# Chunk-by-chunk pooling on GpSimd, side-by-side halves of the mixed attention tiles, and another PSUM layout for the last stage of attention, MoE and a second feed-forward layer

## Chip, cores and metric

The kernel runs on one core of one Trainium2 chip. The metric is the device time of one execution in microseconds; the time before is the median of three runs. One further execution was recorded by the hardware profiler, and every duration below comes from it.

## The reference, cut to what matters

```python
k_p = k.reshape(B, H, Sp, 8, D).mean(axis=3)      # 8 batches, 8 heads, 576 rows -> 72
v_p = v.reshape(B, H, Sp, 8, D).mean(axis=3)
scores = scale * (q @ k_p^T)                      # 576 x 72 for each batch and head
x = softmax(scores) @ v_p                         # -> 4608 tokens x 512
e = argmax(cosine(x, expert_emb) / tau)           # one of 8 experts per token, gate = its softmax weight
x = gate * (relu(x @ w1[e]) @ w2[e])              # first MoE, 512 -> 1024 -> 512
out = max(x @ m1, x @ m2, x @ m3) @ m_out         # second layer, 512 -> 768 -> 512
```

All of it is in float32.

## The kernel before

The work has three stages, and one written order of instructions for each engine. **Attention** goes over 36 tiles of 128 tokens. In a group of nine, tiles 0 to 3 belong to one batch, tile 4 (the mixed one) takes 64 tokens of one batch and 64 of the next, and tiles 5 to 8 belong to the second batch; so tiles 4, 13, 22 and 31 are mixed. An iteration of the loop works on several tiles at once: scores of one (`psc`, L422 and L436), transposed weights of an older one (`paT`, L467), transposed queries of the newest (`pqT`, L411), and weights times V of the oldest (`pav`, `stage_x`, L490). Each of `psc`, `paT` and `pav` has one PSUM buffer, so the next tile's matmuls wait until VectorE or ScalarE has read the last one's.

K and V of a batch come as 576 rows of 8 x 64, in five chunks (four of 128 partitions, one of 64), `kraw` and `vraw`. They are pooled in place in three halving steps, w = 4, 2, 1. For K of batches 0 and 1 VectorE does it; the rest is GpSimd's: `pool_k2` (L263) for K of batches 2 to 7 and `pool_v` (L275) for V of all eight. The four full chunks are done together at each step, `pool_v` taking its first step in two halves, and then the fifth. `spread_v` (L284, instructions at L288) then copies pooled V into the block form `vbd` that `pav` reads. All this stands in one GpSimd queue, and with it the one-hot rows `ohs` (`slot_steps`, L652, L656) of the routing.

The routing's small VectorE instructions (`rank_steps`, L600, through the helpers at L547 to L559 and the copy at L617) are put between the attention's own by `fill` (L910), a few at each place. A chain of them starts after tiles 8, 17 and 23, and another after the last. `early_steps` (L703) multiplies the `ohs` of the first 24 tiles into a list of tokens (`p_early`, L751), with which the first gather of the MoE starts.

**The first MoE** runs over pairs of blocks of 128 tokens of one expert; its matmuls are split in two parts (`hi`, `lo`) of a faster format. **The second layer** (`second`, L1568) takes six groups of 768 tokens, for each of which nine weight chunks go through seven products (`quad`, L1662, matmuls at L1617) in three PSUM tags of the pool `pabc` (L1573), and then an output product into the pool `pout` (L1574). In the first two stages the pools `pq` and `pb` (L117, L118) take PSUM: two banks for `pq`, then six for `psc`, `paT` and `pav`. The last result of the first MoE goes from `paT`'s banks through a transpose into one of `pq`'s (`pyT`, L1126).

Of the kernel before, what the change touches and what calls it, by code (L numbers as in the profile page):

```python
# [14 lines left out]
A = mybir.AluOpType  # L15
AX = mybir.AxisListType.X
PSUM = bass.MemoryType.PSUM
# [4 lines left out]
def attention_moe_moe_kernel(  # L22
# [24 lines left out]
    nc = tc.nc  # L47
    dbg = dbg or {}

    P = 128  # L50
# [38 lines left out]
    def pool(stack, name, bufs, side="left", space=None):  # L89
        kw = {"space": space} if space else {"side": side}  # L90
        return stack.enter_context(tc.tile_pool(name=name, bufs=bufs, reuse_waits="tile", **kw))
# [19 lines left out]
    def bc(ap, shape):  # L111
        return ap.to_broadcast(shape)
# [3 lines left out]
    if True:  # L116
# [61 lines left out]
        if True:  # L178

            RC = [P, P, P, P, 64]  # L180
# [67 lines left out]
            def prep_steps(b):  # L248
                kt, vt = kv[b]
                kb, vb = kbds[b % 3], vbds[b % 3]  # L250
                kp = qp.tile([P, 5, 2, D], F32, tag="kp", name=f"kp{b}")
                vp = kp[:, :, 1, :] if b > 1 else qp.tile([P, 5, D], F32, tag="vp", name=f"vp{b}")
# [8 lines left out]
                        pool_k(c)  # L261

                def pool_k2():  # L263
                    for c0, c1, n in ((0, 4, P), (4, 5, RC[4])):
                        for w in (4, 2, 1):
                            dst = kt[0:n, c0:c1, 0:w, :] if w > 1 else kp[0:n, c0:c1, 0:1, :]
                            nc.gpsimd.tensor_tensor(
                                dst, kt[0:n, c0:c1, 0:w, :], kt[0:n, c0:c1, w : 2 * w, :], op=A.add
                            )

                def dup_k():
                    for c0, c1, n in ((0, 3, P), (3, 4, KC[3]), (4, 5, KC[4])):
                        nc.scalar.copy(kp[0:n, c0:c1, 1, :], kp[0:n, c0:c1, 0, :])

                def pool_v(c0, c1, n):  # L275
                    for w in (4, 2, 1):
                        for a0 in range(c0, c1, 2) if w == 4 else (c0,):
                            a1 = min(a0 + 2, c1) if w == 4 else c1
                            dst = vt[0:n, a0:a1, 0:w, :] if w > 1 else vp[0:n, a0:a1, :].unsqueeze(2)
                            nc.gpsimd.tensor_tensor(  # L280
                                dst, vt[0:n, a0:a1, 0:w, :], vt[0:n, a0:a1, w : 2 * w, :], op=A.add
                            )

                def spread_v():  # L284
                    for c, (h0, h1) in enumerate(HS):
# [188 lines left out]
            AV = []  # L474
# [7 lines left out]
            def stage_x(i):  # L482
                m, part, t, segs = tiles[i]
                aT = st_a.pop(i)
                ps = pb.tile([P, 2, 512], F32, tag="pav", name=f"pav{i}")
                for lo, hi, b in segs:
                    for bank in range(2):
                        parts = [x_ for x_ in AV if x_[1] // 4 == bank]
                        for n, (c, g0, g1, sl) in enumerate(parts):
                            nc.tensor.matmul(  # L490
                                ps[lo:hi, bank, (g0 % 4) * DA : (g0 % 4 + g1 - g0) * DA],
                                aT[0 : RC[c], c, lo:hi],
                                vbds[b % 3][0 : RC[c], sl : sl + g1 - g0, :].rearrange("p h d -> p (h d)"),
                                start=(n == 0),
                                stop=(n == len(parts) - 1),
                                skip_group_check=True,
                            )
                av = ps[:, :, 0 : 4 * DA].rearrange("p a (h d) -> p a h d", d=DA)
                rs = ap2.tile([P, 2, 4, 1], F32, tag="rs", name=f"rs{i}")
                nc.vector.tensor_scalar_add(rs, av[:, :, :, D : D + 1], J * 1e-9)  # L500
                fill(FILL[dense[0]][2])
                nc.vector.reciprocal(rs, rs)
                fill(FILL[dense[0]][3])
                if part == 1 or t % 2 == 0:
                    xg[i] = ap2.tile(
                        [P, 1 if part == 1 else 2, DM], F32, tag=f"x{part % 2}", name=f"x{i}", bufs=2 if part == 1 else 3
                    )
                    xg[i + 1] = xg[i]
                x = xg.pop(i)
                nc.vector.tensor_tensor(  # L510
                    x[:, t % 2, :].rearrange("p (a h d) -> p a h d", a=2, h=4), av[:, :, :, 0:D], bc(rs, [P, 2, 4, D]), op=A.mult
                )
                dt = ap2.tile([P, 2, 4, E], F32, tag="dt", name=f"dt{i}")
                fill(FILL[dense[0]][4])
                nc.vector.tensor_tensor(dt, av[:, :, :, D + 1 : DA], bc(rs, [P, 2, 4, E]), op=A.mult)
                fill(FILL[dense[0]][5])
                nc.vector.tensor_reduce(
                    lg[:, i, :].unsqueeze(2), dt.rearrange("p a h e -> p e (a h)"), axis=AX, op=A.add
                )
                fill(FILL[dense[0]][6])  # L520
                sq = ap1.tile([P, DM], F32, tag="sq", name=f"sq{i}")
                squares.append(
                    lambda: nc.scalar.activation(sq, x[:, t % 2, :], AF.Square, accum_out=ssq[:, i : i + 1])
                )
                if part == 1:
                    r0 = 2 * S * m + 512
                    nc.sync.dma_start(xbuf[r0 : r0 + P, :], x[:, 0, :])
                elif t % 2 == 1:
                    r0 = 2 * S * m + (0 if part == 0 else 640)
                    nc.sync.dma_start(  # L530
                        xbuf[r0 : r0 + 4 * P, :].rearrange("(p t) d -> p (t d)", t=4)[:, (t - 1) * DM : (t + 1) * DM],
                        x.rearrange("p t d -> p (t d)"),
                    )
# [376 lines left out]
            def fill(n=1):  # L910

                for _ in range(n):
                    free = [c_ for c_ in queue[0] if c_.state is None] if queue else []
                    if not free:
                        return
                    c_ = free[0]
                    queue[0].remove(c_)
                    queue[0].append(c_)
                    c_.step()
                    if c_.state == "end":  # L920
                        queue[0].remove(c_)
                        if not queue[0]:
                            queue.pop(0)
# [553 lines left out]
            for it in range(NT + 4):  # L1477
# [33 lines left out]
                if 0 <= it - 4 < NT:  # L1511
                    stage_x(it - 4)
                if it == NT + 1:
                    next(first)
                for job in todo.get(it, []):
# [3 lines left out]
                    b, j = job  # L1519
# [48 lines left out]
    def second(st, groups, again=False):  # L1568
        wq = pool(st, "wstream", 3)
        yp = pool(st, "yin", 2)  # L1570
        t2 = pool(st, "tmp2", 2)
        g1p = pool(st, "gT", 1)
        pa = pool(st, "pabc", 2, space=PSUM)  # L1573
        po_ = pool(st, "pout", 2, space=PSUM)  # L1574
        tl["yr"] = yp
        ghi, glo = (g1p.tile([P, F2C, GW], F32R, name=f"{x_}{groups[0]}") for x_ in ("ghi", "glo"))
        wt, gt, ix = {}, {}, {}
# [162 lines left out]
    with ExitStack() as st:  # L1740
        second(st, list(range(NG)))
# [61 lines left out]
```

## Time and profile before

| | |
|---|---|
| time before, median of 3 runs | 1264.73 us (1262.85 to 1265.89) |
| the profiled execution's own time | 1260.98 us |
| its span, first to last instruction | 1259.2 us |
| TensorE busy | 1215.6 us (97%) |
| VectorE busy | 799.2 us (63%) |
| ScalarE busy | 580.5 us (46%) |
| GpSimd busy | 318.9 us (25%) |
| granted TensorE clock, mean | 0.991 |

PE is TensorE's matmuls, PEld its weight loads, DVE VectorE, ACT ScalarE, POOL GpSimd and SP the engine that issues most DMAs. Attention fills about the first 205 us, the first MoE goes to 701 us, the second layer to the end. A view by window gives the busy time of each engine in a stretch; the timeline lists the instructions in order of time, equal neighbours merged, with the idle time before them and what ended it in square brackets. Of a merged row the time is from the start of its first instruction to the end of its last. A float32 matmul is recorded as two.

### The profile page before, as it was taken

What the parts mean: (1) busy time and instruction counts of PE and PEld (TensorE: products, weight loads), DVE (VectorE), ACT (ScalarE), POOL (GpSimd) and SP (SyncE); (2) the same over time, 40 slices, a digit from 0 to 9 for tenths busy, and PEclk for the clock granted to TensorE, in tenths of its full rate; (3) what the DMA queues carried; (4) which work ended last, traced back from release to release, by engine and by line L of the source; (5) the groups of instructions that cost most, each with busy time, mean ns of one, the idle gap of its engine ahead of it and who ended that gap; (6) DMA issues with size and microseconds to landing.
All of it is one profiled execution on the core that took longest, in us unless ns stands there. A gap on an engine that the chain in (4) does not pass through costs nothing. (4 is left out here: it accounts for less than half of the span.)

```text
span 1259.2 us, 22318 instructions
## 1 busy us (share of the span) xinstructions
PE 1215.6 (97%) x8251; PEld 1158.0 (92%) x8251; DVE 799.2 (63%) x1575; ACT 580.5 (46%) x1040; POOL 318.9 (25%) x383
## 2 busy tenths in 40 slices
PE   5899899999999999999999999999999999999995
PEld 4788789999999999999999998998998998998994
DVE  6676886797889999898764446345445454454450
ACT  3466465545666676666655333323223323223221
POOL 6985553420212212222000302103103004004001
PEclk9899999999999999999999999999999999999998
DMA  9968246423976445844619666475564673773721
GB/s 252 267 202 236 97 138 217 151 85 32 298 262 226 164 143 203 283 151 137 207 51 350 241 238 242 160 262 205 207 239 182 220 264 153 258 263 124 253 108 52
DMA packets 98038, 246.21 MB, mean 196 GB/s; under 512 B 17100, under 2 KB 58106, under 8 KB 89858
## 3 DMA queue, kind: packets, MB, share of 16 engines
q1 hardware_dynamic: 84770, 189.09, 44.5%
q0 software_dynamic: 13152, 55.62, 13.3%
q8 instruction: 67, 1.10, 0.4%
q14 instruction: 49, 0.40, 0.1%
HBM read 252.23 MB, written 46.98 MB: 238 GB/s over the span
## 5 line engine op out<-in xcount | busy, mean ns | idle before, releaser
L1617 PE MATMUL p<-yhi,wt 128*128 128x384 f32 x1512 | 387.2, 336 | 0.0
L1617 PEld LDWEIGHTS p<-yhi,wt 128*128 128x128 f32 x1512 | 273.4, 188 | 0.6
L1617 PE MATMUL p<-ylo,wt 128*128 128x384 f32 x756 | 254.0, 336 | 0.0
L1625 ACT COPY s<-p 128x384 f32<-128x384 f32 x162 | 77.8, 480 | 221.1 <-PE p L1617 216.8
L1104 PE MATMUL py<-hhi,whi 128*128 128x256 f32 x576 | 164.6, 286 | 0.0
L1104 PE MATMUL py<-hhi,wlo 128*128 128x256 f32 x576 | 163.1, 283 | 1.6 <-DVE wlo L1036 1.6
L1056 PE MATMUL ph<-xhi,whi 128*128 128x256 f32 x576 | 163.8, 284 | 0.7 <-DVE hlo L1072 0.7
L1056 PE MATMUL ph<-xhi,wlo 128*128 128x256 f32 x576 | 163.0, 283 | 0.7 <-DVE wlo L1036 0.7
L1056 PE MATMUL ph<-xlo,whi 128*128 128x256 f32 x576 | 163.0, 283 | 0.0
L1104 PE MATMUL py<-hlo,whi 128*128 128x256 f32 x576 | 162.9, 283 | 0.0
L1617 PEld LDWEIGHTS p<-ylo,wt 128*128 128x128 f32 x756 | 142.1, 188 | 0.5
L1646 DVE TENSOR_TENSOR blk<-p,s 128x384 f32<-128x384 f32 x108 | 59.7, 553 | 113.9 <-PE p L1617 113.9
L1602 POOL DMA_INDIRECT gt<-gbuf,ix x26 | 37.0, 1424 | 312.1 <-DMA ix<-idbuf 305.7
L1104 PEld LDWEIGHTS py<-hhi,wlo 128*128 128x128 f32 x576 | 110.4, 192 | 1.8 <-DVE wlo L1036 1.8
L1056 PEld LDWEIGHTS ph<-xhi,whi 128*128 128x128 f32 x576 | 110.5, 192 | 1.2 <-DVE hlo L1072 0.9
L1056 PEld LDWEIGHTS ph<-xhi,wlo 128*128 128x128 f32 x576 | 110.5, 192 | 0.9 <-DVE wlo L1036 0.9
L1056 PEld LDWEIGHTS ph<-xlo,whi 128*128 128x128 f32 x576 | 110.5, 192 | 0.0
L1104 PEld LDWEIGHTS py<-hlo,whi 128*128 128x128 f32 x576 | 110.5, 192 | 0.0
L1104 PEld LDWEIGHTS py<-hhi,whi 128*128 128x128 f32 x576 | 110.4, 192 | 0.0
L1036 DVE TENSOR_TENSOR wlo<-w2raw,whi 128x1024 fp32r<-128x1024 f32 x84 | 102.2, 1221 | 8.8 <-ACT whi L1034 8.7
L1036 DVE TENSOR_TENSOR wlo<-w1raw,whi 128x1024 fp32r<-128x1024 f32 x67 | 81.8, 1220 | 27.6 <-ACT whi L1034 26.5
L1034 ACT CAST whi<-w2raw 128x1024 fp32r<-128x1024 f32 x88 | 91.8, 1044 | 7.7 <-PE py L1104 4.7
(316 smaller groups left out, 2280.8 us busy)
## 6 DMA issues: line engine op xcount, KB each, us to landing
wt<-wdram SPq DMA_DIRECT2D x51, 1792.0 KB
w1raw<-in_moe_w_dram SPq DMA_DIRECT2D x88, 512.0 KB
w2raw<-in_moe_w_dram SPq DMA_DIRECT2D x88, 512.0 KB
wdram<-wst POOLq DMA_DIRECT2D x9, 1792.0 KB
ybuf<-yo SPq DMA_DIRECT2D x40, 256.0 KB
cvraw<-in_moe_w_dram POOLq DMA_DIRECT2D x36, 256.0 KB
vraw<-in_v_dram SPq DMA_DIRECT2D x8, 1024.0 KB
xbuf<-x SPq DMA_DIRECT2D x16, 512.0 KB
```

The source lines that it names most:

```text
L1034: nc.scalar.copy(hi, src)
L1036: eng.tensor_tensor(lo, src, hi.bitcast(F32), op=A.subtract)
L1056: nc.tensor.matmul(ps[:, f, :], a_[:, c, fs], b_[:, c, :], start=(n == 0), stop=(n == 3 * DC - 1))
L1104: nc.tensor.matmul(py[:, c // 2, (c % 2) * 256 : (c % 2 + 1) * 256], a_[:, f, c * P : (c + 1) * P], b_[:, f, :], start=(piece == 0 and f = ...
L1602: nc.gpsimd.indirect_dma_start(out=gt[g][:, j : j + 1], out_offset=None, in_=gbuf[:, :], in_offset=bass.IndirectOffsetOnAxis(ap=cols[j], a ...
L1617: nc.tensor.matmul(ps, a_, b_, start=(start and c + n == 0), stop=(c == 1 and n == 2), skip_group_check=True)
L1625: nc.scalar.copy(t, ps)
L1646: tt(src, add[0], add[1], op=A.add)
```

## The change

Three edits. `pool_k2` and `pool_v` now finish one chunk (three steps on at most 128 partitions x 256 elements) before the next. `stage_x` has its loop over the two halves of a mixed tile innermost, so that the halves alternate, and a tile with one batch keeps its order. `second` opens the pool `pout` ahead of `pabc`, so that `pout` takes PSUM's first two banks and `pabc` the other six.

```diff
--- before.py
+++ after.py
@@ -261,25 +261,20 @@
                         pool_k(c)
 
                 def pool_k2():
-                    for c0, c1, n in ((0, 4, P), (4, 5, RC[4])):
+                    for c, n in enumerate(RC):
                         for w in (4, 2, 1):
-                            dst = kt[0:n, c0:c1, 0:w, :] if w > 1 else kp[0:n, c0:c1, 0:1, :]
-                            nc.gpsimd.tensor_tensor(
-                                dst, kt[0:n, c0:c1, 0:w, :], kt[0:n, c0:c1, w : 2 * w, :], op=A.add
-                            )
+                            dst = kt[0:n, c, 0:w, :] if w > 1 else kp[0:n, c, 0:1, :]
+                            nc.gpsimd.tensor_tensor(dst, kt[0:n, c, 0:w, :], kt[0:n, c, w : 2 * w, :], op=A.add)
 
                 def dup_k():
                     for c0, c1, n in ((0, 3, P), (3, 4, KC[3]), (4, 5, KC[4])):
                         nc.scalar.copy(kp[0:n, c0:c1, 1, :], kp[0:n, c0:c1, 0, :])
 
                 def pool_v(c0, c1, n):
-                    for w in (4, 2, 1):
-                        for a0 in range(c0, c1, 2) if w == 4 else (c0,):
-                            a1 = min(a0 + 2, c1) if w == 4 else c1
-                            dst = vt[0:n, a0:a1, 0:w, :] if w > 1 else vp[0:n, a0:a1, :].unsqueeze(2)
-                            nc.gpsimd.tensor_tensor(
-                                dst, vt[0:n, a0:a1, 0:w, :], vt[0:n, a0:a1, w : 2 * w, :], op=A.add
-                            )
+                    for c in range(c0, c1):
+                        for w in (4, 2, 1):
+                            dst = vt[0:n, c, 0:w, :] if w > 1 else vp[0:n, c : c + 1, :]
+                            nc.gpsimd.tensor_tensor(dst, vt[0:n, c, 0:w, :], vt[0:n, c, w : 2 * w, :], op=A.add)
 
                 def spread_v():
                     for c, (h0, h1) in enumerate(HS):
@@ -483,10 +478,10 @@
                 m, part, t, segs = tiles[i]
                 aT = st_a.pop(i)
                 ps = pb.tile([P, 2, 512], F32, tag="pav", name=f"pav{i}")
-                for lo, hi, b in segs:
-                    for bank in range(2):
-                        parts = [x_ for x_ in AV if x_[1] // 4 == bank]
-                        for n, (c, g0, g1, sl) in enumerate(parts):
+                for bank in range(2):
+                    parts = [x_ for x_ in AV if x_[1] // 4 == bank]
+                    for n, (c, g0, g1, sl) in enumerate(parts):
+                        for lo, hi, b in segs:
                             nc.tensor.matmul(
                                 ps[lo:hi, bank, (g0 % 4) * DA : (g0 % 4 + g1 - g0) * DA],
                                 aT[0 : RC[c], c, lo:hi],
@@ -1570,8 +1565,8 @@
         yp = pool(st, "yin", 2)
         t2 = pool(st, "tmp2", 2)
         g1p = pool(st, "gT", 1)
+        po_ = pool(st, "pout", 2, space=PSUM)
         pa = pool(st, "pabc", 2, space=PSUM)
-        po_ = pool(st, "pout", 2, space=PSUM)
         tl["yr"] = yp
         ghi, glo = (g1p.tile([P, F2C, GW], F32R, name=f"{x_}{groups[0]}") for x_ in ("ghi", "glo"))
         wt, gt, ix = {}, {}, {}
```

GpSimd's queue, at the pooling of K of batch 2 (`kraw` and its result in `kp`), with the semaphores waited for: first before, whole, then the change, its first four chunks of five.

```order
L267 TENSOR_TENSOR kraw_254<-kraw_254 128x4x256 [waits DMAHW4_49,DMAHW3_49,DMAHW5_49,DMAHW2_49,DVE_49]
L267 TENSOR_TENSOR kraw_254<-kraw_254 128x4x128 [waits Pool_49]
L267 TENSOR_TENSOR kp_484<-kraw_254 128x4x64 [waits PE_49,Pool_49]
L267 TENSOR_TENSOR kraw_254<-kraw_254 64x256 [waits DMAHW3_49]
L267 TENSOR_TENSOR kraw_254<-kraw_254 64x128 [waits Pool_49]
L267 TENSOR_TENSOR kp_484<-kraw_254 64x64 [waits Pool_49]
```

```order
L267 TENSOR_TENSOR kraw_262<-kraw_262 128x256 [waits DMAHW4_49,DMAHW3_49,DMAHW5_49,DMAHW2_49,DVE_49]
L267 TENSOR_TENSOR kraw_262<-kraw_262 128x128 [waits Pool_49]
L267 TENSOR_TENSOR kp_500<-kraw_262 128x64 [waits PE_49,Pool_49]
L267 TENSOR_TENSOR kraw_262<-kraw_262 128x256
L267 TENSOR_TENSOR kraw_262<-kraw_262 128x128 [waits Pool_49]
L267 TENSOR_TENSOR kp_500<-kraw_262 128x64 [waits Pool_49]
L267 TENSOR_TENSOR kraw_262<-kraw_262 128x256
L267 TENSOR_TENSOR kraw_262<-kraw_262 128x128 [waits Pool_49]
L267 TENSOR_TENSOR kp_500<-kraw_262 128x64 [waits Pool_49]
L267 TENSOR_TENSOR kraw_262<-kraw_262 128x256
L267 TENSOR_TENSOR kraw_262<-kraw_262 128x128 [waits Pool_49]
L267 TENSOR_TENSOR kp_500<-kraw_262 128x64 [waits Pool_49]
```

Six instructions became fifteen. Second and third steps wait for GpSimd's own instruction before them, and a chunk's first step does not. For V seven instructions became fifteen.

TensorE's queue, at `pav` of the first mixed tile, before and then in the change; `vbd_154` and `vbd_155` are the two batches, and so the two halves.

```order
L490 MATMUL pav_707<-vbd_154,aT_638 64x146
L490 MATMUL pav_707<-vbd_154,aT_638 64x219
L490 MATMUL pav_707<-vbd_154,aT_638 64x73
L490 MATMUL pav_707<-vbd_154,aT_638 64x146
L490 MATMUL pav_707<-vbd_154,aT_638 64x219
L490 MATMUL pav_707<-vbd_154,aT_638 64x73
L490 MATMUL pav_707<-vbd_155,aT_638 64x146
L490 MATMUL pav_707<-vbd_155,aT_638 64x219
L490 MATMUL pav_707<-vbd_155,aT_638 64x73
L490 MATMUL pav_707<-vbd_155,aT_638 64x146
L490 MATMUL pav_707<-vbd_155,aT_638 64x219
L490 MATMUL pav_707<-vbd_155,aT_638 64x73
```

```order
L485 MATMUL pav_757<-vbd_154,aT_688 64x146
L485 MATMUL pav_757<-vbd_155,aT_688 64x146
L485 MATMUL pav_757<-vbd_154,aT_688 64x219
L485 MATMUL pav_757<-vbd_155,aT_688 64x219
L485 MATMUL pav_757<-vbd_154,aT_688 64x73
L485 MATMUL pav_757<-vbd_155,aT_688 64x73
L485 MATMUL pav_757<-vbd_154,aT_688 64x146
L485 MATMUL pav_757<-vbd_155,aT_688 64x146
L485 MATMUL pav_757<-vbd_154,aT_688 64x219
L485 MATMUL pav_757<-vbd_155,aT_688 64x219
L485 MATMUL pav_757<-vbd_154,aT_688 64x73
L485 MATMUL pav_757<-vbd_155,aT_688 64x73
```

The same twelve matmuls stand there, and now each is followed by its counterpart of the other half. Nothing else moves on TensorE, and nothing on VectorE, ScalarE or SP.

## Rows read from the trace of the kernel before

**Rows 1.** The page's first part: busy time, share of the span, instructions.

```profile
PE 1215.6 (97%) x8251; PEld 1158.0 (92%) x8251; DVE 799.2 (63%) x1575; ACT 580.5 (46%) x1040; POOL 318.9 (25%) x383
```

**Rows 2.** Stretches: length, then busy PE, PEld, DVE, ACT, POOL; PEclk, DMA share, GB/s.

```profile
81.40:93.60 12.20, 9.56 (x80) 8.58 (x78) 11.42 (x28) 6.03 (x17) 9.96 (x13) 1.00 0.38 120
125.80:142.20 16.40, 11.57 (x81) 9.90 (x78) 15.94 (x25) 7.08 (x19) 15.69 (x21) 0.90 0.33 111
93.60:125.80 32.20, 32.20 (x242) 28.98 (x241) 21.79 (x61) 21.36 (x55) 17.65 (x23) 1.00 0.81 239
```

**Rows 3.** VectorE's groups by shape, 79 to 142 us: busy us, mean ns.

```profile
L547 DVE TENSOR_TENSOR pre<-pre 128x72 f32<-128x72 f32 x8 | 7.0, 872 | 0.0
L547 DVE TENSOR_TENSOR oh<-w,wm 128x72 f32<-128x72 f32 x2 | 4.4, 2176 | 0.0
L617 DVE COPY pre<-oh 128x72 f32<-128x72 f32 x2 | 4.0, 2000 | 0.0
L551 DVE TENSOR_SCALAR lg<-lg,rtau 128x72 f32<-128x72 f32 x2 | 1.6, 821 | 0.0
L556 DVE SCALAR_TENSOR_TENSOR wt<-lg,w 128x72 f32<-128x72 f32 x2 | 1.1, 570 | 0.1
...
L547 DVE TENSOR_TENSOR rk<-rk,oh 128x72 f32<-128x72 f32 x1 | 0.2, 223 | 0.0
```

**Rows 4.** VectorE's timeline, two instructions of the second rank chain: start, duration.

```profile
129.57 3.92 DVE L547 TENSOR_TENSOR oh<-w,wm 128x72 f32<-128x72 f32 x1
...
137.08 2.62 DVE L547 TENSOR_TENSOR pre<-pre 128x72 f32<-128x72 f32 x1
```

**Rows 5.** GpSimd's timeline: batch 2's pooling, and a spread with batch 7's.

```profile
35.42 3.69 POOL L267 TENSOR_TENSOR kraw<-kraw 128x1024 f32<-128x1024 f32 x2
...
39.88 1.25 POOL L267 TENSOR_TENSOR kraw<-kraw 64x256 f32<-64x256 f32 x2
41.20 0.31 POOL L267 TENSOR_TENSOR kp<-kraw 64x64 f32<-64x64 f32 x1
41.48 3.83 POOL L280 TENSOR_TENSOR vraw<-vraw 128x512 f32<-128x512 f32 x3
...
47.66 3.70 POOL L267 TENSOR_TENSOR kraw<-kraw 128x1024 f32<-128x1024 f32 x2
...
129.06 2.04 POOL L288 TENSOR_TENSOR vbd<-kp,mslot 128x128 f32<-128x128 f32 x5
131.06 3.67 POOL L267 TENSOR_TENSOR kraw<-kraw 128x1024 f32<-128x1024 f32 x2
```

**Rows 6.** TensorE's timeline: a mixed `pav`, a plain one; mixed scores, plain ones.

```profile
57.96 3.63 PE L490 MATMUL pav<-vbd,aT 128*64 128x146 f32 x24
...
112.43 2.00 PE L490 MATMUL pav<-vbd,aT 128*128 128x146 f32 x12
...
83.72 1.35 PE L422 MATMUL psc<-kbd,qT 128*64 128x144 f32 x16 [0.20 <-ACT qT L412]
...
115.42 1.25 PE L436 MATMUL psc<-kbd,qT 128*128 128x144 f32 x8
```

**Rows 7.** GpSimd's timeline, the one-hot rows, with the idle time before them.

```profile
107.76 7.04 POOL L656 TENSOR_SCALAR ohs<-iof,slot,tokid 128x128 f16<-128x128 f32 x9 [15.49 <-DVE slot L556]
...
156.38 0.79 POOL L656 TENSOR_SCALAR ohs<-iof,slot,tokid 128x128 f16<-128x128 f32 x1 [13.04 <-DVE slot L556]
...
174.19 4.99 POOL L656 TENSOR_SCALAR ohs<-iof,slot,tokid 128x128 f16<-128x128 f32 x6 [5.62 <-DVE slot L556]
```

**Rows 8.** TensorE's timeline: the matmuls that read the one-hot rows.

```profile
181.04 0.75 PE L751 MATMUL p_early<-ohbe,ohs 128*128 128x10 f16 x24
```

**Rows 9.** TensorE's timeline near the start: a wait for queries.

```profile
40.69 0.63 PE L411 MATMUL pqT<-ident,qgrp 128*128 128x128 f32 x4 [2.88 <-DMA qgrp<-in_q_dram]
```

**Rows 10.** TensorE's timeline where the second layer begins.

```profile
700.79 0.66 PE L1126 MATMUL pyT<-ident,yr 128*128 128x128 f32 x4 [0.68 <-ACT yr L1097]
701.33 0.41 PE L1617 MATMUL p<-yhi,wt 128*128 128x384 f32 x1
```

## The prediction, made before the changed kernel ran

> **What bounds the kernel now.** I began with the page's busy times: TensorE works 97% of the span [rows 1], 1215.6 of 1259.2 us, so there are 43.6 us of idle TensorE to win, and beyond that only shorter TensorE work. Then I took busy times by window over the attention. Between 93.6 and 125.8 us TensorE is busy all the time; in the two stretches beside it, it idles for 12.20 - 9.56 = 2.64 us and 16.40 - 11.57 = 4.83 us, and VectorE is the full engine there (11.42 of 12.20, 15.94 of 16.40) [rows 2]. In the second one the granted clock is 0.90: the 1.2 GHz level for about 3.3 us of the 16.4, after TensorE had waited, which costs half of 3.3, some 1.6 us more. Together the two stretches cost 9.1 us.
>
> What fills VectorE there? Its groups by shape answer: five kinds of small routing instructions, 16 in all on 128 x 72 elements, take 7.0 + 4.4 + 4.0 + 1.6 + 1.1 = 18.1 us, though one on the same shape takes 0.22 when nothing disturbs it [rows 3]. So 18.1 - 16 x 0.22 = 14.6 us are waiting that the profile books as work. The timelines of VectorE and GpSimd, side by side, say on whom: `oh` runs from 129.57 to 133.49 [rows 4], and GpSimd runs its five spread instructions from 129.06 to 131.06 and the first step of batch 7's K after them (two steps in 3.67 us) [rows 5]. VectorE got in where the second step had to wait for the first. A `pre` of 2.62 us in the same chain is another such case [rows 4]. I read this as a shared way into memory that GpSimd keeps through a run of instructions without a wait between them.
>
> **Pooling chunk by chunk.** The three steps of a fifth chunk, which has the new size of 256 elements a partition, go from 39.88 to 41.48, thus 1.60 us, the last of them 0.28 [rows 5]. In the changed order only a chunk's second and third step wait for the step before. Dividing the other 1.32 us by size, I estimate 0.8 and 0.5 us. A VectorE instruction then meets either a run of 0.28 + 0.8 = 1.08 us (a last step and the next chunk's first) or one of 0.5 us. For an instruction that comes at any moment the mean wait is (1.08 x 1.08 + 0.5 x 0.5) / (2 x 1.6) = 0.44 us, and 16 of them wait 7.0 us instead of 14.6. Before, TensorE saw 7.5 us of the 14.6 as idle time (2.64 + 4.83) and VectorE's own slack took the other 7.1. What is left would fit that slack if it were spread evenly; since it won't be quite, I leave TensorE 1.1 of the 9.1 us. **Gain 8.0 us.** The ends: 9.1 if nothing of it reaches TensorE; and a loss of 3.0 if each of the 16 meets the longest run (17.6 us against 14.6).
>
> The Trainium skill ("SBUF — State Buffer", its rules on the shared port pair) has it that whichever of VectorE and GpSimd starts first holds the pair for its whole instruction, and the other waits. By that, `oh` would have got in after one spread instruction and not after all of them and a pooling step, so the trace shows longer holding than the page. By the page's rule alone the mean wait would be 0.30 us, the whole 9.1 us would come back, and the sum below would be 1.1 us larger.
>
> The price is GpSimd's time. K of batch 2 took 41.48 - 35.42 = 6.06 us and V 47.66 - 41.48 = 6.18 [rows 5]; both become 5 x 1.60 = 8.0. Batch 0's V is hidden by the wait for batch 1's data; six times 1.94 for K and seven times 1.82 for V make 24.4 us. The cover is GpSimd's idle time ahead of the one-hot rows: 15.49 + 13.04 + 5.62 = 34.2 us [rows 7]. But those waits are for VectorE, and if attention comes 8.0 us and three mixed tiles (below, 1.5 each) earlier, 12.5 us of the cover go: 21.7 are left, and the last one-hot rows come 2.7 us late against the rest. They end at 174.19 + 4.99 = 179.18 and are read at 181.04 [rows 7, 8], which leaves 1.9. **Loss 0.8 us**, as a wait ahead of `p_early`; between 0 and 2.7. Nearer needs have more room: no other reader of pooled K and V comes within 5 us of GpSimd's later times, as I carried them along the timeline.
>
> The first V pooling also frees a buffer 1.8 us later, and behind that load on SP's queue stand the queries for which TensorE waits at 40.69 [rows 9]. The DMA engines are saturated then and hold earlier loads in their queues, so I put that at nothing; without that cover it would cost up to 1.8 us once.
>
> **Halves side by side.** A mixed `pav` takes 3.63 us for 24 records, a plain one 2.00 for 12 of twice the width: run one after the other, half as wide costs as much apiece [rows 6]. The scores of mixed tiles already alternate their halves, and there 16 records take 1.35 us where 8 plain ones take 1.25 [rows 6]: two matmuls on different halves run together, for 8% more. So the new `pav` should take 2.00 x 1.08 = 2.16, and save 1.47 in each of four tiles. VectorE waits for each mixed `pav`, and TensorE has work behind it, so the saving lies on the path. **Gain 5.9 us**; ends 0 (accumulating chains don't overlap) and 4 x 1.63 = 6.5.
>
> **The banks.** The first product of the second layer starts at 701.33, right behind the transpose that ends about then (700.79 plus 0.66) [rows 10], and it waits for nothing. The new place only lets other old tiles stand under the tags, all read by then, and no product uses a bank that it shares with a reader later. **Nothing**, either way; the 0.68 us wait ahead of the transpose stays.
>
> **The sum**: 8.0 - 0.8 + 5.9 = 13.1 us. Against the profiled execution's own 1260.98 that is 1247.9. That execution lies 3.75 us below the median of the runs shown, so for the median I take 1264.73 - 13.1 = **1251.6 us**.
>
> **Rivals.** *GpSimd becomes the bound* (slower). From 27 us until the one-hot rows it would hardly rest. 65 chunk triples stand in that line (five for each of 13 poolings), so 0.1 us more for a triple makes `p_early`, and all behind it, 6.5 us later. At 1.80 us instead of 1.60 the whole gain is gone, and at 2.0 the time is 1264.73 - 13.1 + 26 = 1277.6. Against it: the fifth chunk's triple is the same work on as many elements. For it: 30 ends of instructions per batch at which VectorE may step in, instead of 13.
>
> *The waits only spread out.* If contested instructions wait as long in sum as before, the pooling gains nothing and only the halves are left: 1264.73 - 5.9 = 1258.8. For it: GpSimd is busy longer, so more is contested. Against: runs of 2.4 us and more are what rows 4 show.
>
> *The halves don't overlap.* Then 8.0 us remain and GpSimd isn't late: 1256.7. For it: unlike the scores, these add up in one bank. Against it: mixed scores use the same halves of the array.
>
> *The change doesn't reach the end*: TensorE's time is taken up by VectorE or ScalarE soon after, 1264.7. Against it: behind 142 us TensorE is nearly always the one that others wait for.
>
> **Numbers.** Chances: the forecast 0.72, halves alone 0.10, pooling alone 0.09, GpSimd as bound 0.05, nothing 0.04. The first's own range goes from both full gains, 15.6 us, to half of them, 6.5. The range to state also takes in the two partial cases (up to 1258.8) and, at the low end, the 3.75 us by which one execution already lay below the median: 1264.73 - 15.6 - 3.75 = 1245.4. So 1245 to 1259, leaving out under 0.2. A measurement of this kernel tells about 0.2%, 2.5 us, from no change: faster 0.91, same 0.04, slower 0.05.
>
> **What would show it.** Right: the first four groups of rows 3 near 0.6 us a piece at most, both stretches of rows 2 with under 1 us of idle TensorE and clock 1.00, mixed `pav` near 2.2 us, K and V pooling 8.0 us each, `p_early` some 12 us earlier with at most a short wait for GpSimd, the second layer's part unchanged in length. Wrong: triples over 1.7 us, a long wait ahead of `p_early`, mixed `pav` still near 3.6, or VectorE's small instructions still above 1 us.

## The result and the profile after

In the first comparison the changed kernel takes 1249.16 us (median of 4 runs, 1247.23 to 1252.42) and the kernel before 1264.99 us (4 runs). The ratio is 0.988, with a 95% interval of 0.9852 to 0.9908: faster, by about 15.8 us. In the second comparison (`e6_changed_again`) it is 0.9881 (0.9858 to 0.9904). The profiled execution of the changed kernel took 1247.23 us with a span of 1245.5 us. The forecast was 1251.6 us (1245 to 1259).

The changed code is shorter, so the line numbers of the attention are 5 lower than before (`pav` L485, `psc` L417 and L431, `p_early` L746, GpSimd's `pool_k2` L267, `pool_v` L277, spread L283 and `ohs` L651, VectorE's helpers L542 to L554).

The first part of the changed kernel's page, busy time and instructions of each engine:

```profile
PE 1206.5 (97%) x8251; PEld 1151.5 (92%) x8251; DVE 794.2 (64%) x1575; ACT 580.5 (47%) x1040; POOL 339.3 (27%) x501
```

Against [rows 1], GpSimd has 118 instructions and 20.4 us more, and TensorE is 9.1 us less busy with the same number of instructions.

TensorE's timeline shows a mixed `pav`, a plain one, and the queries for which it waited before:

```profile
40.87 0.60 PE L406 MATMUL pqT<-ident,qgrp 128*128 128x128 f32 x4
...
54.87 1.86 PE L485 MATMUL pav<-vbd,aT 128*64 128x146 f32 x24
...
112.36 2.00 PE L485 MATMUL pav<-vbd,aT 128*128 128x146 f32 x12
```

The mixed tile's 24 records now take 1.86 us, less than the plain tile's 12 of twice the width. Before, they took 3.63 [rows 6]: 1.77 us less in each of four tiles. The queries' wait of 2.88 us [rows 9] is gone.

The windows that answer to the two stretches of [rows 2] (length, then busy PE, PEld, DVE, ACT, POOL; clock, DMA share, GB/s):

```profile
76.00:88.00 12.00, 11.80 (x97) 10.60 (x94) 9.84 (x29) 8.30 (x24) 10.82 (x23) 1.00 0.61 185
116.00:127.00 11.00, 10.80 (x90) 9.87 (x89) 9.73 (x29) 7.30 (x22) 9.98 (x21) 1.00 0.59 198
```

In each of them TensorE idles for 0.20 us where it had idled for 2.64 and 4.83, at full clock, though GpSimd pools beside it for nine tenths of the time. VectorE's groups by shape, 75 to 126 us, answer to [rows 3] (busy us, mean ns of one):

```profile
L542 DVE TENSOR_TENSOR pre<-pre 128x72 f32<-128x72 f32 x8 | 3.3, 414 | 0.0
...
L551 DVE SCALAR_TENSOR_TENSOR wt<-lg,w 128x72 f32<-128x72 f32 x2 | 1.0, 496 | 0.1
L612 DVE COPY pre<-oh 128x72 f32<-128x72 f32 x2 | 0.9, 441 | 0.0
...
L542 DVE TENSOR_TENSOR oh<-w,wm 128x72 f32<-128x72 f32 x2 | 0.6, 304 | 0.0
L546 DVE TENSOR_SCALAR lg<-lg,rtau 128x72 f32<-128x72 f32 x2 | 0.6, 289 | 0.0
```

The 16 instructions take 3.3 + 1.0 + 0.9 + 0.6 + 0.6 = 6.4 us instead of 18.1. With 0.22 us of work in each, as the prediction took it, 2.9 us of waiting are left of 14.6. (0.22 is the shortest `pre`. The shortest `oh`, copy and `wt` of these chains are 0.30, 0.32 and 0.37 us, in the changed kernel or in `e4_step_by_step` below, so some 0.7 us of either figure is work and not waiting.)

GpSimd's price shows in its timeline: one chunk of batch 4's V, and its last one-hot rows, with batch 7's spread ahead of them:

```profile
79.93 1.25 POOL L277 TENSOR_TENSOR vraw<-vraw 128x256 f32<-128x256 f32 x2
81.27 0.32 POOL L277 TENSOR_TENSOR kp<-vraw 128x64 f32<-128x64 f32 x1
81.54 1.26 POOL L277 TENSOR_TENSOR vraw<-vraw 128x256 f32<-128x256 f32 x2
...
153.56 6.24 POOL L651 TENSOR_SCALAR ohs<-iof,slot,tokid 128x128 f16<-128x128 f32 x8
159.78 2.06 POOL L283 TENSOR_TENSOR vbd<-kp,mslot 128x128 f32<-128x128 f32 x5
161.84 4.93 POOL L651 TENSOR_SCALAR ohs<-iof,slot,tokid 128x128 f16<-128x128 f32 x6
```

A triple takes 81.54 - 79.93 = 1.61 us. Of the idle time that stood ahead of the one-hot rows [rows 7] nothing is left in these rows. VectorE and TensorE at the same time:

```profile
159.71 2.16 DVE L548 TENSOR_SCALAR texc<-texc 128x8 f32<-128x8 f32 x1
```

```profile
159.10 2.07 PE L485 MATMUL pav<-vbd,aT 128*128 128x146 f32 x12 [0.46 <-DVE pinc L554]
...
164.07 1.17 PE L417 MATMUL psc<-kbd,qT 128*64 128x144 f32 x14 [2.84 <-DVE sh L449]
...
168.04 0.83 PE L746 MATMUL p_early<-ohbe,ohs 128*128 128x10 f16 x24
```

`texc`, 128 x 8 elements, is held from 159.71 to 161.87 us, just as long as the spread of batch 7 lasts (159.78 to 161.84). Behind it on VectorE come the instructions for the softmax, and TensorE waits 2.84 us for them. Before, these scores had no wait above 0.38 us.

Where the time came from is best read as the lead of the changed kernel over the one before, at the same instruction of the two TensorE timelines:

| instruction on TensorE | before, us | after, us | lead, us | what happened since the line above |
|---|---|---|---|---|
| `pav` of tile 3 | 52.81 | 49.72 | 3.1 | the start: no wait for queries, no slow clock after it (see the text) |
| `pav` of tile 11 | 93.60 | 86.25 | 7.4 | mixed tile 4: 1.8; first stretch of rows 2: 2.5 |
| `pav` of tile 20 | 142.16 | 126.38 | 15.8 | mixed tile 13: 1.8; second stretch: 6.7 |
| `pav` of mixed tile 22, start | 150.98 | 135.13 | 15.9 | |
| `p_early` | 181.04 | 168.04 | 13.0 | mixed tile 22: 1.8; the last routing chain: -4.6 |
| first product of the first MoE | 205.50 | 191.10 | 14.4 | mixed tile 31: 1.8; slow clock left from the waits: -0.4 |
| first product of the second layer | 701.33 | 687.24 | 14.1 | |
| last instruction | 1259.2 | 1245.5 | 13.7 | |

So the gain is 3.1 (start) + 7.1 (four mixed tiles) + 9.2 (two stretches) - 5.0 (last chain and its aftermath) = 14.4 us by the end of attention, of which 13.7 last to the end. The first of these terms is not the change's alone: the start also differs between two executions of the same attention (see the start, under the experiments). The medians differ by some 2 us more than the two profiled executions: before's profiled one lay 4.0 us below its median, after's 1.9.

### The profile page after: what moved, and what is told of

Its sections match the earlier page's. It is cut to its first block, busy times and chain, and to the rows that moved or that the text cites. A ratio compares the mean times of both kernels' runs of the same rounds, so it can differ in the third digit from the quotient of the medians.

```text
span 1245.5 us, 22435 instructions
## 1 busy us (share of the span) xinstructions
PE 1206.5 (97%) x8251; PEld 1151.5 (92%) x8251; DVE 794.2 (64%) x1575; ACT 580.5 (47%) x1040; POOL 339.3 (27%) x501
## 3 DMA queue, kind: packets, MB, share of 16 engines
q0 software_dynamic: 13152, 55.62, 13.4%
```

## The experiments

The theory under test: small VectorE instructions come to a shared way into memory only where GpSimd has to wait for its own previous instruction; chunk by chunk, such a wait comes at every second and third step. Each experiment starts from the kernel before or the changed one, and the ratio is always to the kernel before, measured beside it.

**One part at a time.** `e1_pool_alone` is the kernel before with the new `pool_k2` and `pool_v` alone, its other lines as they were:

```diff
                 def pool_k2():
-                    for c0, c1, n in ((0, 4, P), (4, 5, RC[4])):
+                    for c, n in enumerate(RC):
                         for w in (4, 2, 1):
...
                 def pool_v(c0, c1, n):
-                    for w in (4, 2, 1):
-                        for a0 in range(c0, c1, 2) if w == 4 else (c0,):
+                    for c in range(c0, c1):
+                        for w in (4, 2, 1):
...
```

> Only the pooling is chunk by chunk; mixed halves and banks as before. My theory (GpSimd keeps the shared way through a run of instructions without a wait, short triples let VectorE in): the two stretches after tiles 8 and 17 lose their 2.64 and 4.83 us of idle TensorE and the clock returns to 1.00 there (9.1 us), the wait for queries near 40 us with the slow clock behind it goes as in the changed kernel (3.1 us), and because attention reaches the one-hot rows 5 us later than in the changed kernel, less is lost there: 1265 - 12 = 1253 us, between 1251 and 1256. Rival (the halves did most of it, the waits only spread out): 1260 or more.

Measured: 1250.14 us against 1264.95, ratio 0.9872 (0.9827 to 0.9917), a little below the expected 1251 to 1256.

`e2_halves_alone` is the kernel before with the new loop order of `stage_x` alone:

```diff
-                for lo, hi, b in segs:
-                    for bank in range(2):
-                        parts = ...
-                        for n, (c, g0, g1, sl) in enumerate(parts):
+                for bank in range(2):
+                    parts = ...
+                    for n, (c, g0, g1, sl) in enumerate(parts):
+                        for lo, hi, b in segs:
```

> Only the mixed tiles' halves alternate; pooling and banks as before. Theory: a mixed pav takes 1.86 us instead of 3.63, 1.77 us less in each of four tiles, all of it on the path: 1265 - 7.1 = 1258 us, with both idle stretches and the wait for queries as before. Rival (the saving is taken up again by VectorE's full stretches behind tiles 8 and 17): 1261 to 1264.

Measured: 1257.97 us, ratio 0.9942 (0.9918 to 0.9965). TensorE's timeline of this kernel has the short mixed tile, and the first stretch of [rows 2] still has its wait:

```profile
88.39 2.26 PE L436 MATMUL psc<-kbd,qT 128*128 128x144 f32 x8 [2.44 <-DVE pre L547]
...
100.81 1.86 PE L490 MATMUL pav<-vbd,aT 128*64 128x146 f32 x24
```

`e3_banks_alone` only opens `pout` ahead of `pabc`:

```diff
+        po_ = pool(st, "pout", 2, space=PSUM)
         pa = pool(st, "pabc", 2, space=PSUM)
-        po_ = pool(st, "pout", 2, space=PSUM)
```

> Only the second layer's PSUM pools change places. Theory: nothing, 1265 within 2.5 us, the first product of the second layer starts within 0.3 us of where it stood against the last transpose. Rival: it takes a wait away there and gains 0.5 us or more, or adds one.

Measured: 1264.33 us, ratio 0.9998 (0.9976 to 1.0019).

What follows: by these medians pooling gives 14.8 us, the halves 7.0, and the banks nothing that can be told. Together the first two are 21.8, where the whole change gives 15 to 16; by the spans of the profiled executions (1248.9 and 1254.0 us against 1259.2) it is 10.3 + 5.2 = 15.5 against 13.7. So some of the gain overlaps; how much is not settled, with runs of the kernel before between 1259 and 1271 us here. The timelines show one place of it: at the last routing chain, from mixed tile 22 to `p_early`, `e1_pool_alone` loses 1.5 us of its lead, the whole change 4.6. Another part isn't the parts' own doing: tile 3 comes 2.9 us earlier with the pooling alone, but also 1.4 with the halves alone and 2.6 with the banks alone, and neither of these two changes anything that runs before tile 3.

**Is it the size or the waits?** `e4_step_by_step` is the changed kernel with the same 15 small instructions for each pooling, in the other order: all chunks' first steps, then all second steps, then all third ones. Each instruction is as short as in the changed kernel, but a step's operands were finished several instructions ago.

```diff
-                    for c, n in enumerate(RC):
-                        for w in (4, 2, 1):
+                    for w in (4, 2, 1):
+                        for c, n in enumerate(RC):
...
-                    for c in range(c0, c1):
-                        for w in (4, 2, 1):
+                    for w in (4, 2, 1):
+                        for c in range(c0, c1):
```

> The changed kernel with the same small GpSimd instructions in another order: the first step of all chunks, then the second of all, then the third, so that a step hardly ever waits for the instruction just before it. Same number, same sizes, same sum. My theory (VectorE gets in only where GpSimd's next instruction has to wait for its own last one): runs of four or five instructions up to 3 us long, VectorE's 16 routing instructions wait as long as before or longer, the idle stretches after tiles 8 and 17 come back, 1256 us or more. Rival (the way is held for one instruction only, so short instructions are what counts): as the changed kernel, 1249 within 2 us.

Measured: 1268.19 us, ratio 1.0017 (0.9993 to 1.004): all the gain is gone, the halves' included. The 16 instructions of [rows 3] take 20.1 us here, against 18.1 before and 6.4 in the changed kernel. `oh` alone, from VectorE's groups by shape, 80 to 157 us:

```profile
L542 DVE TENSOR_TENSOR oh<-w,wm 128x72 f32<-128x72 f32 x2 | 9.3, 4649 | 0.0
```

GpSimd's timeline, then VectorE's, then TensorE's:

```profile
82.45 2.04 POOL L283 TENSOR_TENSOR vbd<-kp,mslot 128x128 f32<-128x128 f32 x5
84.46 5.50 POOL L267 TENSOR_TENSOR kraw<-kraw 128x256 f32<-128x256 f32 x10
```

```profile
83.50 5.73 DVE L542 TENSOR_TENSOR lg<-lg,mxl 128x72 f32<-128x72 f32 x1
```

```profile
93.75 3.84 PE L485 MATMUL pav<-vbd,aT 128*128 128x146 f32 x12 [7.63 <-DVE dt L510]
...
146.50 3.83 PE L485 MATMUL pav<-vbd,aT 128*128 128x146 f32 x12 [7.10 <-DVE dt L510]
```

One VectorE instruction lasts 5.73 us, through the rest of the spread and most of ten pooling instructions, none of which is a long one (a first step of one chunk takes 0.73 us where the changed kernel's timeline has it alone):

```profile
37.22 0.73 POOL L267 TENSOR_TENSOR kraw<-kraw 128x256 f32<-128x256 f32 x1
```

The rule of the Trainium skill ("SBUF — State Buffer", "SBUF: two separate sides"), by which the other engine waits for the one instruction that holds the pair, would let it in within about 0.7 us. The measurement differs from it, and it decides: with number and sizes the same, the order makes the difference, and not the size. That the wait between a chunk's steps is what lets VectorE in is the reading that fits; no run tried such a wait by itself, and why it should open the way is not shown. The "only" of the theory goes too far: `lg` ends at 89.23, inside a run that goes on without idle time to 89.96 (84.46 + 5.50), so VectorE got in there without a wait of GpSimd's. What ended that hold is open.

**What does GpSimd's lateness cost?** `e5_two_batches_wide` is the changed kernel with batches 3 and 5 pooled the old way. No routing chain meets most of their pooling, and GpSimd is sooner done by the 1.9 us that each of four poolings no longer costs.

```diff
+            WIDE = (3, 5)
...
                 def pool_k2():
+                    if b in WIDE:
+                        for c0, c1, n in ((0, 4, P), (4, 5, RC[4])):
+                            for w in (4, 2, 1):
...
+                        return
                     for c, n in enumerate(RC):
```

and in the same way in `pool_v`.

> The changed kernel, but batches 3 and 5 are pooled in the old wide steps, which frees 2 x 3.8 = 7.6 us of GpSimd where VectorE's routing chains don't run. Theory (the 17.5 us that attention was ahead fell to 13 because GpSimd comes late to the last routing chain: its spread of batch 7, 159.78 to 161.84, stands in VectorE's way, the 2.16 us instruction at 159.71, and its last one-hot rows end late): the spread falls into the gap between VectorE's two bursts, the wait of 2.84 us ahead of the scores at 164 goes, p_early starts 3 to 4.5 us earlier, 1245 us. Rival (GpSimd's load isn't the cause): p_early and the time as in the changed kernel, 1249.

`e6_changed_again` is the changed kernel once more, beside it.

> The changed kernel once more, to stand beside the others on the same chip: 0.988 of the kernel before, within 0.003.

Measured: 1240.85 us for the first (5 runs, 1240.13 to 1244.55), ratio 0.9829 (0.9805 to 0.9853), and 1248.25 for the second, ratio 0.9881. **This version beats both kernels**: by 22 us the one before, by 7.4 us the changed one. GpSimd and TensorE in it (lines 19 higher than in the changed kernel):

```profile
152.21 2.04 POOL L302 TENSOR_TENSOR vbd<-kp,mslot 128x128 f32<-128x128 f32 x5
155.48 4.99 POOL L670 TENSOR_SCALAR ohs<-iof,slot,tokid 128x128 f16<-128x128 f32 x6 [1.22 <-DVE slot L570]
```

```profile
159.35 1.17 PE L436 MATMUL psc<-kbd,qT 128*64 128x144 f32 x14
...
162.33 0.75 PE L765 MATMUL p_early<-ohbe,ohs 128*128 128x10 f16 x24
```

GpSimd waits for VectorE again and not the other way round; these scores no longer wait for VectorE. From the start of mixed tile 22 (134.48) to `p_early` it is 27.9 us, where the changed kernel takes 32.9 (135.13 to 168.04) and the kernel before 30.1, 1.8 of them for the longer mixed tile.

**Through which wait does it cost?** Two more kernels part the spread's place from the lateness itself. `e9_spread_sooner` is the changed kernel with batch 7's spread two iterations sooner:

```diff
+                if b == 7:
+                    at_[1] -= 2
                 for j, t in enumerate(at_):
```

> The changed kernel with batch 7's five spread instructions moved ahead of the eight one-hot rows on GpSimd: they should run near 150.4 to 152.5 us instead of 159.8 to 161.8; GpSimd's work in sum and the end of its last one-hot rows (166.8 us) stay. Theory (the late GpSimd hurts by a spread run that falls on VectorE's last routing chain): no VectorE instruction over 1 us between 155 and 168 us, the 2.84 us wait of TensorE ahead of the scores falls under 1 us. TensorE would then be at p_early near 164.6 us and has to wait there for the one-hot rows, some 2 us, so that only 1 to 2 us are won: 1246 to 1248 us. Rival (the one-hot rows are not what is read last; only the spread counts): p_early at 164.6 us without a wait, 1244.5 us. Other rival (VectorE's chain is simply too much work in that place): a wait of 2 us or more ahead of the scores stays, and the time is the changed kernel's, 1248 to 1249 us.

Measured: 1250.24 us, ratio 0.9877 (0.9848 to 0.9907), 2 us above the expected time and no better than the changed kernel. Its timeline has every step of the theory, though (GpSimd's, then TensorE's):

```profile
150.71 2.04 POOL L283 TENSOR_TENSOR vbd<-kp,mslot 128x128 f32<-128x128 f32 x5
152.70 3.14 POOL L1481 DMA_DIRECT2D ybuf<-ones  x4
155.88 11.34 POOL L651 TENSOR_SCALAR ohs<-iof,slot,tokid 128x128 f16<-128x128 f32 x14
```

```profile
161.32 1.17 PE L417 MATMUL psc<-kbd,qT 128*64 128x144 f32 x14 [0.83 <-DVE sh L449]
...
164.30 0.84 PE L746 MATMUL p_early<-ohbe,ohs 128*128 128x10 f16 x21
165.74 0.18 PE L746 MATMUL p_early<-ohbe,ohs 128*128 128x10 f16 x1 [0.60 <-POOL ohs L651]
166.51 0.18 PE L746 MATMUL p_early<-ohbe,ohs 128*128 128x10 f16 x1 [0.59 <-POOL ohs L651]
167.28 0.18 PE L746 MATMUL p_early<-ohbe,ohs 128*128 128x10 f16 x1 [0.59 <-POOL ohs L651]
```

No VectorE instruction is held for 0.9 us or more between 140 and 172 us, the scores wait 0.83 instead of 2.84, and `p_early` starts at 164.30. Then its last three matmuls wait for the last three one-hot rows. What was not expected stands behind that, in the windows of 164 to 182 us, first of this kernel, then of the changed one:

```profile
164.00:182.00 18.00, 16.20 (x103) 14.79 (x101) 8.48 (x29) 5.98 (x15) 5.06 (x7) 0.72 0.46 147
```

```profile
164.00:182.00 18.00, 17.54 (x145) 15.94 (x146) 13.14 (x47) 9.39 (x25) 4.95 (x6) 0.91 0.48 160
```

After these small waits the granted clock is 0.72 over 18 us, against 0.91: 0.56 of the stretch at the 1.2 GHz level against 0.18, which is (0.28 - 0.09) x 18 = 3.4 us of full-speed time lost. With the three waits that is more than was won: from the start of mixed tile 22 to that of mixed tile 31 this execution takes 51.5 us and the changed kernel's 47.1. By the ratios of the medians the two kernels are the same.

`e10_one_batch_wide` has one wide batch instead of two:

```diff
-            WIDE = (3, 5)
+            WIDE = (5,)
```

> The changed kernel with batch 5 alone pooled the old, wide way: GpSimd comes to its one-hot rows 3.8 us sooner (1.94 for K and 1.82 for V), half of what two wide batches gave. Theory (the late GpSimd is the whole loss at the last routing chain): the last one-hot rows end near 163 us, p_early comes between 163 and 165 us, and the time lies between the two kernels, 1242 to 1246 us. Rival (what counts is only on which VectorE instruction the spread run falls): the spread comes near 156 us, in the middle of the chain, holds an instruction there for 2 us all the same, and the time is 1246 to 1249 us.

Measured: 1246.99 us, ratio 0.9856 (0.9827 to 0.9886), between the two kernels and 1 us above the theory's range. At the last chain it behaves as the theory says: 140.09 to 167.74, 27.7 us from mixed tile 22 to `p_early`, as quick as with two wide batches, without a wait over 0.4 us. The rival's spread (157.79 us) holds nothing back. What keeps the time up is another place: batch 5's wide pooling now runs into the end of the first routing chain (VectorE, then TensorE), and the granted clock over 97 to 115 us, the wait within, is 0.81. The wait of 2.10 us and the clock, 0.19 x 18 = 3.4 us, make up the 5.6 us by which tile 20 comes later than with two wide batches (131.34 and 125.72).

```profile
97.94 2.64 DVE L659 CAST lb<-ri 128x9 f32<-128x9 int32 x1
```

```profile
100.86 2.97 PE L504 MATMUL pav<-vbd,aT 128*128 128x146 f32 x12 [2.10 <-DVE slot L570]
```

With batch 3 wide too, that pooling comes 5.8 us sooner (its first step at 86.15 and not at 91.99 us) and no VectorE instruction between 90 and 102 us takes a microsecond. So half the edit is worth little, and which batches are pooled wide has to be chosen by what VectorE does at that time.

**The start.** The lead of 3.1 us at tile 3 was not forecast. `e7_queries_early` is the kernel before with the queries of tiles 5 to 8 loaded ahead of batch 2's K and V; `e8_wide_and_early` adds this to `e5_two_batches_wide`.

```diff
                 while kvnext < B and kvnext * 4.5 - 11 <= it:
...
+                    if kvnext == 1:
+                        load_q(*qorder[qnext])
+                        qnext += 1
                     kvnext += 1
```

> The kernel before, with one load moved: the queries of tiles 5 to 8 go to SP's queue ahead of batch 2's K and V. Theory (the 3.1 us that the changed kernel is ahead at tile 3 are the wait of 2.88 us for these queries and the slow clock behind it, a transfer whose arrival and not the pooling sets that point): the wait goes, the clock stays at 1.00 between 41 and 49 us, tile 3 comes 3 to 6 us earlier, 1260 us. Rival (VectorE's long constant instruction near 34 us is what holds tile 1 up, so the queries' arrival doesn't matter): 1265 and TensorE waits for VectorE there instead.

> Both edits on the changed kernel: batches 3 and 5 wide, queries early. Theory: the gain of the wide batches stays, 1245 us, and the earlier queries add nothing, since the changed kernel no longer waits for them (tile 5's are there when TensorE comes). Rival: the start is set by the transfers as a whole, K and V of batches 1 and 2 come later and it loses 1 to 3 us.

Measured: 1262.19 us for the first, ratio 0.9989 (0.9976 to 1.0002), no change that can be told; 1241.01 for the second, ratio 0.9838 (0.9805 to 0.9871), the same as without it. In `e7_queries_early` the wait for queries is gone, but TensorE waits a little sooner, for VectorE:

```profile
32.66 3.83 DVE L551 TENSOR_SCALAR thq<-iof 128x13 f32<-128x13 f32 x1
```

```profile
37.21 0.46 PE L422 MATMUL psc<-kbd,qT 128*64 128x144 f32 x2 [2.78 <-DVE sh L454]
```

`thq`, a constant on 128 x 13 elements, lasts 3.83 us, while GpSimd runs a spread and a pooling step. Tile 3 comes 1.7 us sooner, and that doesn't reach the end so that it could be told. But the edit isn't needed for any of this. `e3_banks_alone`, whose attention is the kernel before's unchanged, shows the same on TensorE:

```profile
36.26 0.46 PE L422 MATMUL psc<-kbd,qT 128*64 128x144 f32 x2 [2.04 <-DVE sh L454]
...
40.60 1.06 PE L411 MATMUL pqT<-ident,qgrp 128*128 128x128 f32 x4
```

It waits for VectorE and not for the queries, and its tile 3 starts at 50.21, 2.6 us sooner than in the profiled execution of the kernel before; by tile 20 (141.16) 1.0 us of that is left. `e2_halves_alone`, the same up to tile 4, has no wait for queries either, waits 3.08 us for VectorE at 36.27 and starts tile 3 at 51.41. So the start comes out differently from one execution to the next, and one pair of traces can't tell what the queries or the pooling do to it. Taken together, the three kernels with the old pooling and the loads in their old order start tile 3 at 50.21 to 52.81, and the six that pool the first batches chunk by chunk at 48.48 to 49.95. So the change seems to gain something there; how much isn't settled. The changed kernel has its waits too, in another place: TensorE waits 3.15 us for VectorE at 30.39.

## Why the prediction held, and where its terms were off

**The pooling** (8.0 us forecast for the two stretches): 9.2 us came back, all of it; measured against the trace of `e3_banks_alone`, whose attention is the kernel before's, it is 10.7. The mechanism, GpSimd's runs holding VectorE up, was right, and `e4_step_by_step` shows that the run counts and not the size of its instructions. The size was a little too careful: the mean wait estimated at 0.44 us was at most 2.9 / 16 = 0.18 us, so only 0.2 us of idle time were left in each stretch, where 1.1 us had been kept. The estimate took VectorE to arrive at any moment of a triple; many of the instructions met no wait at all. The triple of 1.60 us was 1.61, and K and V took 8.1 us each, as forecast. One bound was worked out wrong, without effect on the sum: 16 x 1.08 is 17.3 and not 17.6, so the low end was a loss of 2.7 us.

**The halves** (5.9 us, upper end 6.5): 7.1 us, above the stated upper end. The step that failed is "2.00 x 1.08 = 2.16": the scores' ratio of 1.08 isn't the one that holds for `pav`. A mixed `pav` takes 0.93 of a plain one. I had taken the plain tile's 2.00 us as a floor for the mixed one, and no row said so.

**GpSimd's lateness** (-0.8 us, ends 0 and -2.7): -4.6 us until `p_early` and -0.4 behind it, far outside its ends. The place was right, the last one-hot rows, and so was the reason, GpSimd's cover eaten up by its own work and by an earlier attention. What failed is "as a wait ahead of `p_early`": the delayed queue of GpSimd also carries a spread run, which came to lie on VectorE's last chain and held it for 2 us, and TensorE's clock fell after the waits. When `e9_spread_sooner` takes the spread away, the wait that I had forecast appears, and it costs as much. I had looked at who waits for the late instruction and not at whom the late instructions would disturb. `e5_two_batches_wide` bears out that it is the lateness: with it gone, 7.4 us come back by the medians, and by the timelines 6.1 until the first MoE, 5.1 of them between mixed tile 22 and `p_early`.

**The start** ("I put that at nothing"): 3.1 us gained by this pair of traces, but 0.5 against `e3_banks_alone`. I had only asked what a buffer freed later would cost there. VectorE's constants were held by GpSimd at the start too (`im` 4.04 us at 33.76 in the kernel before), by the mechanism that I had seen in [rows 3], and I had not looked for it outside the two stretches. That this is what the change gains there is argued and not shown.

**The banks** (nothing): nothing that the total shows. The first product starts 0.71 us behind its transpose's start instead of 0.54 [rows 10]. In `e3_banks_alone` it is 0.70, and every other kernel has 0.55 or 0.70 to 0.71 according to which of the two places it uses, so the new place costs some 0.16 us once; why was not looked into.

Put together, the terms that were too small (1.2 for pooling, 1.2 for the halves, 3.1 at the start) and the one that was too small a loss (4.2) nearly cancel: 13.1 us forecast, 13.7 us by the profiled executions (1247.9 us forecast for such a one, 1247.2 measured). Against the trace of `e3_banks_alone` the parts up to the first MoE are 0.5 + 7.1 + 10.7 - 5.0 = 13.4 with rounding, so the start and the stretches can't be parted to better than 2 us, and their sum is 12.3 or 11.2. The mechanisms of pooling and halves held; that the total came so near was luck, since a loss six times the forecast one (5.0 for 0.8) was made up by gains that the sum did not have.

Of the rivals, *the waits only spread out* is refuted by the 16 instructions' 6.4 us, *the halves don't overlap* by the 1.86 us, *the change doesn't reach the end* by the lead of 13.7 us that is left at the last instruction. *GpSimd becomes the bound* was the nearest to happening: its triple is 1.61 us and not 1.80, but in the last chain it is the bound, for 5 us.

## What to carry to other kernels

When a small instruction of one engine shows ten times its usual duration, look at what the other engine of the pair runs at that moment, and count its back-to-back run and not its single instruction. Breaking that run up with dependent steps cures it at a price in the other engine's time, so pay it only where the two meet: here two batches less gave another 7 us. And when a change makes an engine late, ask not only who waits for it, but also onto whose work its later instructions will fall.

## What the runs showed of the hardware that was not expected

- Two 64-column halves in turn, each adding up in its own partitions of a bank, take 1.86 us for 24 matmuls, less than 12 matmuls of full width over the same columns (2.00 us), and half of 24 one after the other (3.63 us).
- VectorE is held through long stretches of a run of GpSimd's spread and pooling instructions when none of them waits for the one before: 5.73 us in `e4_step_by_step`. Yet the one-hot rows, which also run back to back, let it in: in `e9_spread_sooner` a run of 14 takes 11.34 us, and no VectorE instruction in it lasts 0.9 us. One of these, a `tensor_tensor` like the held `lg` and `oh`, begins and ends within a single row:

```profile
157.52 0.78 POOL L651 TENSOR_SCALAR ohs<-iof,slot,tokid 128x128 f16<-128x128 f32 x1
157.67 0.41 DVE L542 TENSOR_TENSOR pinct<-pf,tri 128x64 f32<-128x64 f32 x1
```

What tells the two kinds apart was not tried.
- In `e9_spread_sooner` three waits of 0.6 us for one-hot rows, behind 2.3 us of other waits since 157 us, were followed by 18 us at a mean granted clock of 0.72 (more than half of it at the 1.2 GHz level): 5.0 us of speed lost behind some 4 us of waiting. The changed kernel waited 0.46, 2.84 and 0.38 us from 158 to 166 us, nearly as long in sum, and its clock over the same 18 us was 0.91, 1.6 us lost. So the sum of the waits doesn't tell the price; what does was not tried.
